# Attention ends one step sooner beside a pair, and the next pair's q, k, v are asked for in the step that it leaves

## Chip, cores and metric

The kernel runs on one core of one Trainium2 chip. The metric is the time of one execution on the device in microseconds (us), as the median of the runs of one kernel; lower is better.

## The reference, cut to what matters

```python
# 8 batches, 8 heads, 576 tokens, head width 64; chunks of 64 tokens
scores = scale * q_c @ k_c.T          # in each chunk of 64
attn = exp(scores - max); attn /= (sum + 1e-9)
out = attn @ v_c                       # heads joined: x is 4608 x 512
x = (x @ w_a * (x @ w_b)) @ w_out      # 512 -> 1536 -> 512
x = (x @ w1 * (x @ w2)) @ w3 @ w_out2  # 512 -> 1024 -> 1024 -> 512
```

All values are float32. w_a, w_b and the others come as 64-bit floats and are rewritten to float32 in the kernel.

## The kernel before, in words

The 4608 tokens are nine blocks of 512. Blocks 0 to 7 form four pairs (`sb` 0 to 3), block 8 is alone. Phase 0 is attention and the first gated product, phase 1 the second one. A product of float32 values is made of parts of fewer bits, three matmuls for one.

**Stages of phase 0.** Pair 0 goes through plain steps (`plain_step`): one step for each of the 12 slices of 128 hidden columns and each of the two blocks (T = 0 and 1), a pair of products `pa` and `pb` in each. A step with T = 0 also carries the second product (out of the hidden columns, into `acc`) of the slice before; the second products of the T = 1 block are left for a burst. Pairs 1 to 3 go through 12 Strassen steps each (`strassen_step`, `block_steps`): seven products of six matmuls for a slice of both blocks (P5, P1, P2, P6, P3, P7, P4 in this order), and 12 matmuls of the second product of the even block's slice before. The second product of the odd block follows in a burst (`burst`): 12 slices, called blocks of the burst in what follows, of four parts with three matmuls each, 144 matmuls in a row, and the four pending parts of the last step behind its first slice. In the burst the other engines also form the next pair's left factors (`strassen_pieces`).

**Attention.** A unit (`Unit`) is the attention of one block for two heads, eight units for a pair, four for block 8. Its pieces are load1 (q, k), load2 (v), turn (transposes of q and k), scores (32 small matmuls and the maximum), soft2, flip and flip2 (transposes), apply (32 small matmuls and the copies out). Units of pair 1 and before (`TurnedOnPE`) transpose through TensorE, the others on VectorE. `attention_pieces` writes the pieces of all units in one list with a cost for each, and a `Track` spreads the list over a number of points: at each `point()` it lets out pieces until their cost has reached the share of points passed. A Strassen step has 7 points, a burst gives one for each of its slices 4 to 11, a plain step 3 (T = 1) or 5 (T = 0). `finish()` lets out what is left. Attention beside pair 1 is that of pair 2, beside pair 2 that of pair 3, beside pair 3 that of block 8 (there with rewriting of weights, and without points in the burst).

**Loads.** q, k and v are not loaded where a unit asks for them: `ask` puts each small DMA on a list, and `tick(loads=n)` issues the next n of them on SP's queue: 3 ahead of each Strassen product, 1 ahead of each part of a second product (`Second.part`), 2 ahead of each plain product. `settle` issues at once whatever a unit needs by then: a turn calls it for its q and k, an apply for its v. SP also issues the weights (`load_part`, w, two steps ahead) and the second product's weights (`Outs.ahead`, wo, two slices ahead in a step, three in a burst, from four buffers), all in the order of the program. q, k and v have two buffers each, so the first two units of a pair can be loaded ahead (`attention_begins`) when the last two of the pair before have used theirs.

**The lines that matter.** `attention_begins` is called at line 1359, ahead of the burst; for pair 1 the first unit's 16 loads are then issued at once (line 1361). The spread is set in lines 1364 to 1372:

```python
n_pts = PTS * steps + steps - 4      # 7 * 12 + 8 points
at.append(Track(work, n_pts - 3))    # 89
```

In the plain phase the tail of the attention of pair 1 is spread over `4 * (len(order) - n) - 2` points from the first T = 1 step on, which is 82.

Of the kernel before, what the change touches and what calls it, by code (L numbers as in the profile page):

```python
# [78 lines left out]
def chunk_attention_two_gated_products(  # L79
# [66 lines left out]
    def settle(n):  # L146
        while asks["done"] < n and asks["left"]:
            nc.sync.dma_start(*asks["left"].popleft())  # L148
            asks["done"] += 1
# [89 lines left out]
    state = {"banks": ("rB", "rD")}  # L239
# [742 lines left out]
    def ready(ph, j, f, gplaces):  # L982
        return g_parts(gplaces[f // 4][:, f % 4], f"{ph}_{j}b{f}", nc.gpsimd)
# [44 lines left out]
    def attention_begins(units):  # L1028
        for u in units[:2]:
            u.load1()  # L1030
            u.load2()
# [61 lines left out]
    with tc.manual_schedule():  # L1093
# [54 lines left out]
        def unit_list(sb):  # L1148
            js = [LONE] if sb == NSB else [2 * sb, 2 * sb + 1]
            cls = TurnedOnPE if sb == 1 else Unit  # L1150
            return [cls(j, hp, T) for T, j in enumerate(js) for hp in range(NHP)]


        U = [First(T, hp, T) for T in range(2) for hp in range(NHP)]
        for i in range(3):
            pump.load(slot(6), nc.scalar)
# [45 lines left out]
        for n, (T, f) in enumerate(order):  # L1202
            if T == 0:
                conv = Track([conv_piece()] * (1 if f == 0 else 3), 5 if f + 1 < AHEAD else 8)
                if f + 1 == NF[0]:
                    conv = None
            if T == 1 and f == 0:
                late.finish()
                at = Track(both[cut:], 4 * (len(order) - n) - 2)

            def point(pe=True):
                if conv:
                    conv.point(pe)
                (at or late).point(pe)

            if n + 1 == len(order):
                state["ready"] = ready(0, 1, 0, plain[0])
            plain_step(0, 0, T, f, f"0_{T}_{f}", point, plain[0], sums[0], "AC")
            if conv and (T == 1 or f + 1 < AHEAD):
                conv.finish()  # L1220
                pump.flush()
# [17 lines left out]
        def block_steps(ph, sb, x, at):  # L1239

            single = sb == NSB
            j = LONE if single else 2 * sb
            nm = f"{ph}{sb}"
            new = ph == 0 and sb == 1
            whole_new = ph == 1 and sb == 0
            sums, gplaces = [], None if single else []
            n = NF[ph]
            su = first_sums
            last = single
            for f in range(n):  # L1250
                extra = None
                if new:
                    if f + 2 < n:
                        su[f + 2] = summed(ph, f + 2, f + 2)
                        su[f + 2].load()
                    extra = Track(su[f + 1].pieces() if f + 1 < n else [], 5)
                if whole_new:
                    if READY <= f + 2 < n:
                        su[f + 2] = Sums(ph, f + 2, dict(tag=f"Y{f % 2}"))
                        su[f + 2].load()  # L1260
                    if READY <= f + 1 < n:
                        extra = Track(su[f + 1].all_pieces(), 6)

                def freed(i):
                    if f + 2 < n:
                        if whole_new and f + 2 >= READY:
                            return
                        if not new or i in (0, 3):
                            load_part(ph, f + 2, i)
                    elif ph == 0 and sb + 1 == NSB:  # L1270
                        if i < 2:
                            load_plain(ph, f + 2 - n, i)
                    elif not last:
                        load_part(ph, f + 2 - n, i)

                def point(pe=True):
                    if extra:
                        extra.point()
                    for a in at:
                        a.point(pe)  # L1280

                if f + 1 == n and not single:
                    state["ready"] = ready(ph, j + 1, 0, gplaces)
                wo = state["outs"].next()
                strassen_step(ph, j, f, x, f"{nm}_{f}", point, gplaces, sums, wo, freed)
                if extra:
                    extra.finish()
            for a in at:
                a.finish()
            return j, gplaces  # L1290
# [44 lines left out]
        for ph, sb in [(0, sb) for sb in range(1, NSB + 1)] + [(1, sb) for sb in range(NSB + 1)]:  # L1335
            lone = ph == 0 and sb == NSB
            begins = ph == 1 and sb == 0
            if begins:
                state["outs"] = Outs(1, 2 * NSB + 1)
            state["outs"].ahead(2)  # L1340
            if lone:
                x, pieces = lone_pieces(x32, f"{ph}{sb}")
                pieces = pieces + o2_pieces()
                pump.cap = len(pump.jobs)
                slots["n"] = -1
                pieces += [(0.1, False, lambda: pump.load(slot("L")))] * 2
            elif not begins:
                x, pieces = strassen_pieces(x32, f"{ph}{sb}", sb == NSB)
            if ph == 0 and sb == 1:
                for f in range(2):  # L1350
                    first_sums[f] = summed(ph, f, f)
                    first_sums[f].load()
                for f, i in ((0, 0), (0, 3), (1, 0)):
                    load_part(ph, f, i)
                pieces = pieces + first_sums[0].pieces()
            steps, at, conv = NF[ph], [], []
            if ph == 0 and not lone:
                units = unit_list(sb + 1)
                attention_begins(units)
                if sb == 1:  # L1360
                    settle(units[0].qk_end)
                    load_part(ph, 1, 3)
                work = attention_pieces(units)
                n_pts = PTS * steps + steps - 4
                if sb == NSB - 1:
                    pump.cap += 3 * NF[1]
                    pump.load(slot(3))
                    pump.load(slot(3))
                    conv = later_conv(3 * NF[1], 3)
                    work = merged((0, 1, work), (0, 1, conv))  # L1370
                    n_pts = PTS * steps
                at.append(Track(work, n_pts - 3))
            if not begins:
                burst(ph, j + 1, places, pieces, [] if conv else at, state.pop("ready", None))
            if lone:
                got = []
                for n_ in range(4):
                    load_w3(n_)
                at.append(Track(between(got), 5 * steps - 15))
                xs = {}  # L1380

                def next_x():
                    diffs = deque()
                    for i in range(2):
                        t = pool.tile([P, 4, NT], F32, tag=f"G{i}", name=f"xd{i}")
                        diffs.extend(t[:, n_] for n_ in range(4))
                    xs["x"], xs["pieces"] = strassen_pieces(got, "10", diffs=diffs)

                early = [(0.1, False, lambda: (at[0].finish(), next_x()))]
                early += [(0.7, False, lambda n_=n_: xs["pieces"][n_][2]()) for n_ in range(18)]  # L1390
                late = Track(early, 11)
                class After:
                    n = 0

                    def point(self, pe=True):
                        self.n += 1
                        if self.n > 5 * steps - 15:
                            late.point(pe)

                    def finish(self):  # L1400
                        late.finish()

                at.append(After())
                lone_steps(ph, x, at)
                for p in xs["pieces"][18:]:
                    p[2]()
                x32, x = got, xs["x"]
                continue
            if ph == 1 and sb < NSB:
                got = []  # L1410
                js = [LONE] if sb == NSB - 1 else [2 * sb + 2, 2 * sb + 3]
                at.append(Track(x2_pieces(js, got), PTS * steps - 3))
            j, places = block_steps(ph, sb, x, at)
            if ph == 0:
                x32 = [u.x32 for u in units]
            elif sb < NSB:
                x32 = got
# [47 lines left out]
```

## Time and profile before

| | us |
|---|---|
| median of 3 runs | 1654.66 (1654.49 to 1661.31) |
| profiled execution, its own time | 1660.61 |
| its span, first to last instruction | 1658.8 |
| TensorE busy | 1568.2 |
| VectorE busy | 852.7 |
| plain steps, to about | 269 |
| burst, then pair 1 | 269 to 311, to 479 |
| burst, then pair 2 | 479 to 522, to 685 |
| burst, then pair 3 | 685 to 727, to 893 |
| burst, block 8, phase 1 | 893 to 932, to 1095, to 1659 |

Times in the profile are microseconds from the span's start. PE is TensorE, PEld its weight loads, DVE VectorE, ACT ScalarE, POOL GpSimd, SP the engine that issues most DMAs (SPq its queue of issues). L829 is the Strassen product, L858 the second product, L148 the issue of a q, k or v load, L701 of wo, L713 and L715 of w, L467 and L480 transposes through TensorE, L345 the scores, L396 the product with v. In brackets behind an instruction stands how long its engine was idle before it, and what ended that. The granted clock is a share of TensorE's full 2.4 GHz.

### The profile page before, as it was taken

How to read it: one execution, taken by the hardware profiler on the slowest of the kernel's cores; microseconds unless marked ns; L12 is line 12 of the kernel's file. 1: busy time of each engine (PE TensorE's matmuls, PEld its weight loads, DVE VectorE, ACT ScalarE, POOL GpSimd, SP SyncE). 2: the span in 40 equal slices, each digit the busy share in tenths (PEclk: the TensorE clock that was granted, in tenths of full speed). 3: DMA queues.
4: the chain of work that ended last, by engine and by line, in shares of the span. 5: the costliest groups of instructions: out<-in, count | busy, mean ns of one | idle time of the engine just before them, and what ended most of it. 6: DMA issues, size and time to landing. Idle time of an engine off the chain costs nothing.

```text
span 1658.8 us, 24429 instructions
## 1 busy us (share of the span) xinstructions
PE 1568.2 (95%) x8968; PEld 1256.4 (76%) x8968; DVE 852.7 (51%) x1384; ACT 551.8 (33%) x989; POOL 489.7 (30%) x502
## 2 busy tenths in 40 slices
PE   5789999899999999899999899999999999999998
PEld 4568777677776777677777677788878878878887
DVE  5657755777865455645676234544452352342331
ACT  5544444332242222332234222333332332331322
POOL 1213333222252111432224211223432331331432
PEclk8889999999999999999999999999999999999999
DMA  8768876878777777788986888886776676666684
GB/s 222 225 197 268 254 234 190 255 243 240 229 222 212 213 219 211 214 232 299 321 299 216 295 308 303 311 289 247 249 236 213 218 237 211 223 227 200 219 292 160
DMA packets 289975, 400.37 MB, mean 241 GB/s; under 512 B 175680, under 2 KB 196160, under 8 KB 289856
## 3 DMA queue, kind: packets, MB, share of 16 engines
q1 hardware_dynamic: 262688, 309.67, 61.3%
q0 software_dynamic: 23616, 81.80, 12.8%
q10 hardware_dynamic: 3552, 7.34, 1.2%
q8 instruction: 71, 1.16, 0.3%
q14 instruction: 48, 0.39, 0.1%
HBM read 312.74 MB, written 85.98 MB: 240 GB/s over the span
## 4 chain that ended last, share of the span: by engine, by line
PE 75%; DMA 7%; DVE 6%; issue 4%; ACT 3%; SPq 2%; POOL 2%; POOLq 0%; ACTq 0%; DVEq 0%
PE P L829 38%; PE acc L858 19%; PE pa L815 4%; PE pb L815 4%; PE wf L1082 3%; SPq L148 2%; PE pb0L L815 2%; PE pa0L L815 2%; DMA wo<-dwo 2%; PE x L396 1%; DMA cv_w<-in_moe_w_dram 1%; DVE xP L243 1%; DMA qk<-in_q_dram 1%; DMA cv_o<-in_moe_w_out_dram 1%; DVE c L917 1%
## 5 line engine op out<-in xcount | busy, mean ns | idle before, releaser
L829 PE MATMUL P<-xP,w 128*128 128x512 f32 (+1 forms) x3102 | 715.3, 383 | 19.9 <-DVE c L917 12.5
L829 PEld LDWEIGHTS P<-xP,w 128*128 128x128 f32 x3102 | 557.2, 188 | 147.2 <-DVE c L917 18.0
L917 DVE TENSOR_TENSOR c<-P,c 128x512 f32<-128x512 f32 (+1 forms) x228 | 150.5, 662 | 333.2 <-PE P L829 332.2
L914 ACT COPY c<-P 128x512 f32<-128x512 f32 (+1 forms) x228 | 128.6, 564 | 226.4 <-PE P L829 226.1
L945 POOL TENSOR_TENSOR G<-c,c 128x512 f32<-128x512 f32 x68 | 89.4, 1315 | 337.9 <-DVE c L917 337.8
L242 ACT CAST gh<-c 128x512 fp32r<-128x512 f32 x68 | 42.3, 622 | 329.7 <-DVE c L944 329.7
L243 POOL TENSOR_TENSOR gl<-c,gh 128x512 fp32r<-128x512 f32 x68 | 90.2, 1327 | 177.4 <-ACT gh L242 177.4
L858 PE MATMUL acc<-gh,wo 128*128 128x512 f32 x384 | 139.1, 400 | 0.0
L944 DVE TENSOR_TENSOR c<-P,c 128x512 f32<-128x512 f32 x68 | 47.0, 691 | 136.0 <-PE P L829 136.0
L858 PE MATMUL acc<-wo,gh 128*128 128x512 f32 x320 | 111.2, 391 | 0.5 <-ACT gh L242 0.5
L858 PEld LDWEIGHTS acc<-gh,wo 128*128 128x128 f32 x384 | 72.9, 190 | 16.6
L243 DVE TENSOR_TENSOR xP<-xP,xP 128x512 fp32r<-128x512 f32 (+1 forms) x56 | 64.2, 1187 | 25.3 <-ACT xP L242 25.2
L815 PE MATMUL pa<-xq,w 128*128 128x512 f32 x288 | 76.1, 416 | 0.0
L858 PE MATMUL acc<-gl,wo 128*128 128x512 f32 x192 | 75.6, 394 | 0.0
L157 POOL DMA_DIRECT2D dw<-w x58 | 32.5, 560 | 133.0 <-DVE w L243 79.2
L815 PE MATMUL pb<-xq,w 128*128 128x512 f32 x288 | 71.1, 396 | 0.0
L858 PEld LDWEIGHTS acc<-wo,gh 128*128 128x128 f32 x320 | 60.1, 188 | 13.9 <-ACT gh L242 1.0
L815 PEld LDWEIGHTS pa<-xq,w 128*128 128x128 f32 x288 | 57.1, 201 | 13.1
L867 ACT COPY ev<-acc 128x512 f32<-128x512 f32 x72 | 42.4, 589 | 71.8 <-PE acc L858 67.0
L858 PE MATMUL acc<-wo,gl 128*128 128x512 f32 x160 | 63.0, 394 | 0.8 <-POOL gl L243 0.8
L815 PEld LDWEIGHTS pb<-xq,w 128*128 128x128 f32 x288 | 53.0, 188 | 10.9
L1082 PE MATMUL wf<-wo,w3t 128*128 128x512 f32 x192 | 50.2, 421 | 4.8 <-DVE w3t L243 4.6
(154 smaller groups left out, 2327.2 us busy)
## 6 DMA issues: line engine op xcount, KB each, us to landing
w<-dw SPq DMA_DIRECT2D x213, 512.0 KB, 4.3
wo<-dwo SPq DMA_DIRECT2D x168, 512.0 KB, 4.5
dw<-w POOLq DMA_DIRECT2D x58, 512.0 KB, 4.8
w<-dw SPq DMA_DIRECT2D x87, 256.0 KB, 3.4
d<-cv POOLq DMA_DIRECT2D x40, 256.0 KB, 4.7
su<-d SPq DMA_DIRECT2D x20, 512.0 KB, 5.5
cv_o<-in_moe_w_out_dram SPq DMA_DIRECT2D x18, 512.0 KB, 5.8
x2d<-ev POOLq DMA_DIRECT2D x36, 256.0 KB, 4.8
```

The source lines that it names most:

```text
L148: nc.sync.dma_start(*asks["left"].popleft())
L242: nc.scalar.copy(dst_h, src)
L243: eng_l.tensor_tensor(dst_l, src, dst_h, op=ALU.subtract)
L815: nc.tensor.matmul(ps, w[m][:, kk // 2, wp, kk % 2], xq[kk // 2][:, kk % 2, xp], start=(n == 0), stop=(n == 3 * KM - 1),)
L829: nc.tensor.matmul(ps, w[:, wp, kt], x[:, kt, xp], start=(begins and n == 0), stop=(n == 5), skip_group_check=True,)
L858: nc.tensor.matmul(acc[m], a, b, start=(f == 0 and (wp, gp) == SEQ[0]), stop=(f == NF[ph] - 1 and (wp, gp) == SEQ[-1]),)
L867: nc.scalar.copy(t, acc[m])
L914: nc.scalar.copy(t, src)
L917: add = lambda o, a, b: nc.vector.tensor_tensor(o, a, b, op=ALU.add)
L944: nc.vector.tensor_tensor(g, last, c11, op=ALU.mult)
L945: nc.gpsimd.tensor_tensor(g_place(ph, nm.split("_")[0], f, gplaces), c22, c12, op=ALU.mult)
L1082: nc.tensor.matmul(ps, t[:, gp, jj], wo2[jj // 2][:, jj % 2, wp], start=(jj == 0 and (wp, gp) == SEQ[0]), stop=(jj == NF[1] - 1 and (wp, g ...
```

## The change

The first two units of the next pair are made, and their loads asked for, in a function of its own. It is called ahead of the last plain step and ahead of the last Strassen step of pairs 1 and 2, behind a `finish()` of the attention that runs there. The spread is shortened to fit: 78 points in the plain phase, 84 in pairs 1 and 2; pair 3 keeps its 81. The 16 loads that were issued at once ahead of the first burst no longer are.

```diff
+        def next_units(sb):
+            state["units"] = unit_list(sb)
+            attention_begins(state["units"])
...
-                at = Track(both[cut:], 4 * (len(order) - n) - 2)
+                at = Track(both[cut:], 4 * (len(order) - n) - 6)
...
             if n + 1 == len(order):
+                at.finish()
+                next_units(2)
                 state["ready"] = ready(0, 1, 0, plain[0])
...
+                if f + 1 == n and ph == 0 and sb + 1 < NSB:
+                    for a in at:
+                        a.finish()
+                    next_units(sb + 2)
                 if f + 1 == n and not single:
                     state["ready"] = ready(ph, j + 1, 0, gplaces)
...
             if ph == 0 and not lone:
-                units = unit_list(sb + 1)
-                attention_begins(units)
+                units = state.pop("units")
                 if sb == 1:
-                    settle(units[0].qk_end)
                     load_part(ph, 1, 3)
                 work = attention_pieces(units)
-                n_pts = PTS * steps + steps - 4
+                n_pts = PTS * (steps - 1) + steps - 4
...
-                at.append(Track(work, n_pts - 3))
+                at.append(Track(work, n_pts - 1 if sb + 1 < NSB else n_pts - 3))
```

## Rows read from the trace of the kernel before

**Rows 1.** The page, busy time by engine: us (share of the span) xinstructions.

```profile
PE 1568.2 (95%) x8968; PEld 1256.4 (76%) x8968; DVE 852.7 (51%) x1384; ACT 551.8 (33%) x989; POOL 489.7 (30%) x502
```

**Rows 2.** By stretch: length, busy PE, PEld, DVE, ACT, POOL, clock, DMA share, GB/s.

```profile
479.40:522.30 42.90, 39.18 (x191) 30.67 (x190) 32.27 (x38) 18.66 (x34) 21.90 (x18) 0.96 0.78 208
...
515.70:522.30 6.60, 4.63 (x14) 3.54 (x14) 2.36 (x5) 1.71 (x3) 1.11 (x2) 0.74 0.72 191
685.40:727.20 41.80, 37.28 (x160) 29.10 (x159) 26.63 (x27) 18.36 (x33) 21.96 (x18) 1.00 0.90 256
697.00:704.00 7.00, 3.52 (x16) 2.87 (x16) 7.00 (x9) 2.13 (x5) 3.04 (x2) 1.00 0.93 246
...
311.00:479.00 168.00, 161.45 (x1115) 125.96 (x1114) 115.09 (x215) 49.75 (x95) 45.29 (x49) 1.00 0.77 236
522.40:685.00 162.60, 159.80 (x1114) 126.06 (x1113) 79.75 (x152) 38.51 (x72) 32.18 (x26) 1.00 0.73 211
```

**Rows 3.** Timeline of TensorE, burst ahead of pair 2: start, length, instruction, [idle before].

```profile
494.09 0.47 PE L858 MATMUL acc<-gh_3b,wo 128*128 128x512 f32 x1 [0.51 <-DMA wo<-dwo]
...
512.87 0.47 PE L858 MATMUL acc<-gh_3b,wo 128*128 128x512 f32 x1 [0.27 <-DMA wo<-dwo]
...
517.84 0.60 PE L858 MATMUL acc<-gh_3b,wo 128*128 128x512 f32 x1 [1.96 <-DMA wo<-dwo]
```

**Rows 4.** Timeline of TensorE, burst ahead of pair 3.

```profile
700.57 0.47 PE L858 MATMUL acc<-gh_5b,wo 128*128 128x512 f32 x1 [3.48 <-DMA wo<-dwo]
```

**Rows 5.** Waits of TensorE in 311 to 479: us in total, times, longest.

```profile
PE P L829 <- DVE c L917: 3.7, 3, 1.8
PE x L396 <- DVE pT L384: 2.2, 3, 1.2
```

**Rows 6.** Waits of TensorE in 522.4 to 685.

```profile
PE P L829 <- DVE c L917: 2.5, 3, 1.1
```

**Rows 7.** Timeline of TensorE, end of the plain steps.

```profile
231.26 0.69 PE L396 MATMUL x<-pT,v 64*64 64x64 f32 x32 [1.00 <-ACT pT L483]
...
268.55 0.79 PE L396 MATMUL x<-pT,v 64*64 64x64 f32 x32 [0.73 <-ACT pT L483]
```

**Rows 8.** Timeline of SP's issues, burst ahead of pair 2.

```profile
478.98 0.32 SPq L715 DMA_DIRECT2D w<-dw  x1
479.67 0.32 SPq L701 DMA_DIRECT2D wo<-dwo  x1
480.04 4.82 SPq L148 DMA_DIRECT2D qk<-in_q_dram  x8
484.96 0.38 SPq L701 DMA_DIRECT2D wo<-dwo  x1
...
508.50 2.88 SPq L148 DMA_DIRECT2D qk<-in_k_dram  x6
...
513.48 0.54 SPq L701 DMA_DIRECT2D wo<-dwo  x1
```

**Rows 9.** Timeline of SP's issues, burst ahead of pair 3.

```profile
686.57 0.38 SPq L701 DMA_DIRECT2D wo<-dwo  x1
687.04 3.00 SPq L148 DMA_DIRECT2D qk<-in_q_dram  x4
690.08 4.57 SPq L148 DMA_DIRECT2D qk<-in_k_dram  x4
694.75 0.95 SPq L701 DMA_DIRECT2D wo<-dwo  x1
```

**Rows 10.** Instructions on the tile wo in 478 to 525, its loads.

```profile
DMA to landing us min/median/max: 3.6/4.7/6.2
```

**Rows 11.** Timeline of SP's issues, a step of pair 2 with 22 loads.

```profile
593.10 0.37 SPq L715 DMA_DIRECT2D w<-dw  x1
```

**Rows 12.** Timeline of TensorE, the same step.

```profile
586.45 1.66 PE L829 MATMUL P<-xP,w 128*128 128x512 f32 x6 [0.60 <-DVE c L917]
```

**Rows 13.** Timeline of SP's issues, plain steps.

```profile
227.84 2.80 SPq L148 DMA_DIRECT2D qk<-in_k_dram  x4
```

## The prediction

> **What bounds the kernel now.** I read the page first: TensorE is busy for 95% of the span [rows 1], so only its waits and its clock can be gained. Then I read the busy time by stretch, to find the stages next to the change, and in them TensorE's waits. Three stages matter. (a) The bursts, in which TensorE has only the second product of the odd block: 12 blocks of 12 matmuls, each block with its own weights wo. The burst ahead of pair 2 (479.4 to 522.3) and the one ahead of pair 3 (685.4 to 727.2) [rows 2] wait for wo: 0.51, 0.27 and 1.96 us in the one [rows 3], 3.48 us in the other [rows 4]. (b) The twelve-step stages of pairs 1 and 2, where TensorE waits for VectorE [rows 5, 6]. (c) The end of the plain steps, with a wait of 0.73 us ahead of the last attention product [rows 7].
>
> Why wo is late is read in SP's queue. SP issues everything in program order: wo, and among them the small loads of q, k, v, one at each accumulating part. In the burst at 479.4 the wo of block 2 is issued at 479.67, then eight q loads take 4.82 us, and block 3's wo goes out at 484.96; ahead of block 11's wo (513.48) stand eight more, six of them in 2.88 us [rows 8]. In the burst at 685.4 eight loads lie between 687.04 and 694.66, block 3's wo goes out only at 694.75, and that is the wait of 3.48 us [rows 4, 9]. A wo takes 3.6 to 6.2 us, in the median 4.7, from issue to landing [rows 10].
>
> **How late a wo may be.** Block 4 of the first burst would have started at 494.09 - 0.51 = 493.6; matmuls start every 0.22 us (16 in 3.52 us busy, [rows 2]), some 2.7 us for twelve, so block 3 was due at 490.9, 11.5 us after the stage's start, and block 2 one block sooner, 8.7. In the second burst block 3 was due at 697.1, 11.7 after the start, block 2 at 8.9 or a little less.
>
> **Part 1: what is moved.** Counted from the two load functions, a unit of a block that spans two batches (blocks 4 and 6) has 16 q and k loads and 10 of v, a unit of block 8 has 8 and 6. So 52 loads are asked for ahead of pair 2's and of pair 1's burst, 28 ahead of pair 3's. A Strassen step lets out 7 x 3 + 4 = 25 loads, a burst 52 (4 x 12, and 4 in the pending parts). Thus 25 of the 52 and 25 of the 28 go to the pair's last step; in the plain phase the last step has two products of 2 each, so 4. Nothing is removed: the same DMAs, bytes and SP time.
>
> What this costs in the last step: SP is free there now, its last weight load goes out at 478.98 as the step ends [rows 8]. A step with 22 loads ends otherwise: its last product begins at 586.45 and takes 1.66 us, and the weight load that this product frees is issued at 593.10, 5.0 us late [rows 11, 12]. 25 loads at 0.60 us (8 in 4.82) and five larger ones make 16.6 us against 12 us of matmuls (54 x 0.22): 4.6 late; at 0.48 us (6 in 2.88) 13.6, so 1.6 late [rows 8]. I take a lateness L of 4 us when the burst begins, between 1.6 and 5, nearer to the step that does what the new step will do. Those weights are needed only after the burst, so L matters to wo alone.
>
> **Burst ahead of pair 3.** Now 3 loads are left in it, not 28. Block 2's wo went out 1.2 us after the start [rows 9]; it goes out at L + 1.2 = 5.2 and lands at 9.9 to 11.0 (landing 4.7, or the 5.8 from 694.75 to 700.57). Due at 8.9 at the latest: a wait of 1.0 to 2.1, say 1.6. Block 3's follows at 5.2 + 0.4 + 3 x 0.6 = 7.4, lands at 12.1 to 13.2, due at 11.7 + 1.6: none. Before 3.48, after 1.6: **-1.9 us** (between -3.5 at L = 1.6, and -0.9 at L = 5).
>
> **Burst ahead of pair 2.** It has 27 of the 52 left, but from its sixth block the third unit's 16 q and k loads are asked for as now, so 43 of the 52 slots stay in use: the burst is hardly lighter until its last two blocks. Block 3's wo goes out at L + 0.4 + 4.8 = 9.2, lands at 13.9 to 15.0, due at 11.5: it waits about 3.0 us where it did not wait at all (the burst at 685.4 shows this case: issued 9.35 us after its start, 3.48 us of waiting). What goes: the waits 0.51 + 0.27 + 1.96 = 2.74 us, and the slow clock behind the last of them, where 14 matmuls took 4.63 us at a granted clock of 0.74 [rows 2], 1.55 us over 14 x 0.22. The eight loads ahead of block 11's wo become four, since the second unit's loads were all let out before its transposes force them. By block 3 alone the sum is 3.0 - 4.3 = -1.3. By SP's own pace it is less: from block 3's wo to block 11's SP took 28.5 us; with L = 4 in front and four loads (2.4 us) fewer, block 11's wo is 1.6 us later than before, which eats the 1.55 us of the clock. I take **-0.6 us**, from -4.0 (L = 1.6) to +1.8 (L = 5 and a slow clock again). The clock is no sure term: behind the longer wait of 3.48 us the stretch 697 to 704 kept 1.00 [rows 2].
>
> The Trainium skill, "DMA: Bandwidth & Descriptors", section "Issuing engines are not separate DMA queues", says that the time to initiate a DMA is usually small relative to the DMA itself. By that rule neither the old place nor the new one would cost anything. The trace disagrees: 9.35 us pass before one wo can be issued, against a median landing of 4.7 us. By the rule both burst terms would be nought.
>
> **Part 2: the earlier end of attention.** In the plain phase the spread falls from 82 points, of which only 81 exist, to 78. The tail behind the last product (a transpose through TensorE, a copy, 32 small matmuls with the 0.73 us wait [rows 7]) moves into the step before: -0.7. Against it, the last unit's turn comes one and a half steps sooner, to the end of the step that now ends with the attention product at 231.26 [rows 7]. That unit's k loads are issued until 227.84 + 2.80 = 230.6 [rows 13]; with a landing like wo's least, 3.6 us, they are there at 234.2, and TensorE, in order, would wait at about 232: 2.2 us; nothing if the counts let them go 2 loads earlier and the 1 us wait that is there now absorbs the rest. I take +1.3, together **+0.6 us** (-0.7 to +1.7).
>
> In pairs 1 and 2 the spread goes from 89 points to 84, 6% denser, and the last step has none. Scores, transposes, sums and products are the same number and keep their length. What can change is how often a piece stands in VectorE's queue ahead of an add that TensorE needs: the waits are 3.7 + 2.2 us in the one stage [rows 5] and 2.5 in the other [rows 6], 8.4 in all; 6% of them is 0.5. I take **+0.6 us**, between -2 and +3, since each wait is a coincidence of a piece and a product, and all of these shift.
>
> **Part 3: the forced issue.** Ahead of pair 1's burst 16 loads were forced out together; now 12 of them are spread in it. In the old place SP stood waiting for a weight buffer anyway, and that burst used all 52 slots before and uses 52 after. I put it at nothing; cover is the second unit's transposes, which now find their last load just issued instead of 12 loads ahead. Without cover VectorE waits one landing, up to 4.7 us, and TensorE only what is left of it at the next scores: 0 to 1 us.
>
> **Sum.** -1.9 - 0.6 + 0.6 + 0.6 = -1.3 us. It is made against the profiled execution, 1660.61 us with a span of 1658.8 (1.8 us around it); that one is 6.0 us above the median of the runs, 1654.66. I take the difference off the median: 1653.4 us.
>
> **The rivals.**
> A. Bursts clean (18%): L is near 1.6, because the last step has no attention and no loads waiting for buffers, which the 22-load step had. Then -3.5, -4.0 and the tail's -0.7: -8.2, so 1646.5 us. For it: VectorE and SP have nothing else in that step; against it: 25 x 0.60 us does not fit into 12 us.
> B. Slower (27%): SP's lateness is carried into the burst and grows. The place is the first blocks of both bursts, the price 1 us per us of L in each. It decides from L = 5.3 in the first burst (L - 1.0 against 4.3) and about 5.9 in the second; at L = 8 the two are +2.7 and +2.1, with the 1.2 of part 2 +6.0: 1660.7 us. For it: the step with only 22 loads already ends 5.0 us late; against it: that step began with loads waiting for buffers.
> C. Nothing moves (5%), as if issue time were free: both burst terms nought and part 2 nought, 1654.7 us. Against it stands the 3.48 us behind eight loads.
> The forecast, between -5 and +1.5, has 50%.
>
> **Range.** 1645 to 1661 us takes in A's and B's prices and all but about 2 in 10; the forecast's own range is 1649.5 to 1656. A measurement can tell some 0.5%, 8.3 us, from no change. Over 0.5% faster needs A and a gain in the pair stages too: 10%. Over 0.5% slower needs B at L = 8 and worse pair stages: 7%. Within: 83%.
>
> **What would show it.** Right: 25 q, k, v loads in the last step of pairs 1 and 2, the last weight load there some 4 us behind its product; no wait of about 3.5 us at block 3 of the burst ahead of pair 3, but one of 1 to 2 us at block 2; in the burst ahead of pair 2 a wait near block 3, none of 2 us at block 11; a wait for k at the last unit's turn near 232 us. Wrong: bursts without any wait for wo (A), bursts that are longer than 42.9 and 41.8 us (B), or stages of pairs 1 and 2 that differ by over 3 us from 168.0 and 162.6 [rows 2].

## The result, and the profile after

The changed kernel takes 1672.07 us in the median (1665.81 to 1673.06, 5 runs) against 1654.66 in the same job: a ratio of 1.0081, interval [1.0059, 1.0102], so 13.4 us slower (9.8 to 16.9, the ratio times 1654.66). Forecast were 1653.4 us and a range of 1645 to 1661; "slower by over 0.5%" had been given 7%. The profiled execution has a span of 1671.0 us, 12.2 more than before. TensorE is as busy as it was, so the time is waits and clock:

```profile
PE 1569.8 (94%) x8968; PEld 1258.9 (75%) x8968; DVE 850.4 (51%) x1384; ACT 551.6 (33%) x989; POOL 487.3 (29%) x502
```

Stage by stage, from the first matmul of a stage to the first of the next, in us (worked out from TensorE's timelines):

| stage | before | after | the kernel before once more (e8) |
|---|---|---|---|
| to the end of the plain steps | 269.3 | 273.4 | 267.6 |
| burst, pair 1 | 41.6, 168.6 | 41.6, 172.8 | 41.9, 168.6 |
| burst, pair 2 | 42.8, 163.4 | 45.6, 159.7 | 40.9, 163.5 |
| burst, pair 3 | 41.4, 166.9 | 45.7, 169.8 | 40.5, 165.6 |
| burst, block 8, phase 1 | 38.1, 162.9, 563.8 | 39.0, 159.4, 564.0 | 37.8, 163.0, 563.7 |

The plain steps, pairs 1 and 3 and two bursts lost 3 to 4 us each; pair 2 and the stage of block 8 won 3.7 and 3.5. (The 2.9 us in pair 3 are not explained; in the other traces here it takes 165.1 to 168.1.) The busy time by stretch answers [rows 2]; columns as there. In order: the burst ahead of pair 2 and the stretch behind its wait; the burst ahead of pair 3, its wait and the stretch behind it; pairs 1 and 2; a stretch in pair 1.

```profile
487.90:533.50 45.60, 39.05 (x189) 30.32 (x188) 30.76 (x38) 18.65 (x34) 19.93 (x18) 0.93 0.79 221
502.00:510.00 8.00, 7.48 (x25) 5.62 (x26) 5.03 (x8) 2.32 (x5) 1.30 (x1) 0.81 0.82 212
693.20:738.90 45.70, 37.12 (x157) 30.27 (x156) 26.55 (x27) 18.24 (x33) 19.79 (x18) 0.93 0.75 237
704.00:710.00 6.00, 0.00 (x0) 0.00 (x0) 6.00 (x8) 0.65 (x2) 1.80 (x2) 0.70 0.97 344
710.00:720.00 10.00, 9.87 (x37) 8.06 (x38) 4.13 (x4) 2.81 (x5) 2.75 (x2) 0.84 0.63 224
315.00:487.80 172.80, 163.48 (x1117) 127.98 (x1117) 116.76 (x215) 50.06 (x95) 45.41 (x49) 0.99 0.78 233
533.60:693.20 159.60, 159.28 (x1117) 126.56 (x1116) 81.24 (x153) 38.60 (x73) 32.43 (x27) 1.00 0.73 207
396.00:406.00 10.00, 6.71 (x24) 5.22 (x23) 7.62 (x13) 1.21 (x2) 2.64 (x2) 0.83 0.72 226
```

**The bursts.** TensorE's timeline in the two bursts answers [rows 3, 4]: one long wait for wo in each, at the burst's block 2 (the 0.52 and 0.25 us ahead of pair 2 are at its blocks 4 and 8).

```profile
501.97 0.77 PE L858 MATMUL acc<-gh_3b,wo 128*128 128x512 f32 x1 [5.76 <-DMA wo<-dwo]
509.76 0.47 PE L858 MATMUL acc<-gh_3b,wo 128*128 128x512 f32 x1 [0.52 <-DMA wo<-dwo]
522.03 0.47 PE L858 MATMUL acc<-gh_3b,wo 128*128 128x512 f32 x1 [0.25 <-DMA wo<-dwo]
...
710.13 0.77 PE L858 MATMUL acc<-gh_5b,wo 128*128 128x512 f32 x1 [8.58 <-DMA wo<-dwo]
```

The wait of 1.96 us at block 11 is gone, as forecast, and two longer ones came in front. Why is in SP's timeline, which answers [rows 8, 9]: the last step of pair 1, then that of pair 2.

```profile
476.05 5.40 SPq L148 DMA_DIRECT2D qk<-in_q_dram  x8
481.50 0.43 SPq L148 DMA_DIRECT2D qk<-in_k_dram  x1
482.03 0.41 SPq L713 DMA_DIRECT2D w<-dw  x1
...
493.68 0.53 SPq L715 DMA_DIRECT2D w<-dw  x1
494.25 0.47 SPq L148 DMA_DIRECT2D v<-in_v_dram  x1
494.82 0.64 SPq L701 DMA_DIRECT2D wo<-dwo  x1
...
683.45 4.15 SPq L148 DMA_DIRECT2D qk<-in_k_dram  x4
...
700.43 0.95 SPq L715 DMA_DIRECT2D w<-dw  x1
701.42 0.59 SPq L148 DMA_DIRECT2D v<-in_v_dram  x1
702.06 1.17 SPq L173 DMA_DIRECT2D cv_o<-in_moe_w_out_dram  x2
703.33 0.38 SPq L701 DMA_DIRECT2D wo<-dwo  x1
```

The last weight load (L715) can go out when the step's last product frees its buffer; that product ended at 487.35 and 692.68; it goes out at 493.68 and 700.43. SP is 6.3 and 7.8 us late, and block 2's wo goes out 6.9 and 10.1 us after the bursts' starts (487.9 and 693.2). Of the 25 loads 24 stand ahead of that weight load; in SP's rows they take 15.2 us in the one step and 16.4 in the other, 0.63 and 0.68 each. Most issues take 0.3 to 0.7 us. The rest is waits of SP for earlier loads to land, in the one step above all (1.4 us for a wo is the longest), and single long issues: of the four k loads in 4.15 us, one took 2.31. On the chain of waits (start, length, what) these two wo also take longer than the median of [rows 10]:

```profile
494.82 7.02 DMA wo<-dwo
...
703.33 6.67 DMA wo<-dwo
```

The second of them is no longer than before the change. Behind two rewriting loads (L173), block 2's wo ahead of pair 3 took 6.2 to 8.8 us to land in every trace here; in the kernel before, for the one issued at 686.57:

```profile
DMA to landing us min/median/max: 6.7/6.7/6.7
```

Block 2's wo ahead of pair 2 landed in 3.9 to 5.2 us in the other traces.

Behind both waits TensorE's clock is low: 37 matmuls took 9.87 us in 710 to 720 at a granted clock of 0.84, 25 took 7.48 us in 502 to 510 at 0.81. In TensorE's timeline the first seven behind each wait start some 0.43 us apart, the following ones 0.23: half the clock, 1.2 of 2.4 GHz, and 1.5 us lost in each burst.

**Pair 1.** VectorE's transpose of k waits for its load, the add behind it in VectorE's queue is late, a product waits, and the clock falls to 0.83 in 396 to 406 (1.4 us on 24 matmuls). In the trace before VectorE never waited for q or k there. The product with v also waits longer for VectorE's transposes (L396, released by L384): 4.5 us in the five traces with 84 points beside pair 1, e1's among them, against 2.2 in the nine others [rows 5]. That part is the spread alone.

```profile
397.59 0.71 DVE L334 STREAM_TRANSPOSE kT<-qk 128x512 f32<-128x512 f32 x1 [3.16 <-DMA qk<-in_k_dram]
```

```profile
399.53 2.93 PE L829 MATMUL P<-xP,w 128*128 128x512 f32 x6 [3.29 <-DVE c L917]
```

**Plain steps.** Transposes through TensorE now wait in two places, each at the turn of a unit; the 0.73 us at the tail [rows 7] is still there, one step earlier. TensorE's waits in 105 to 269 us (total, times, longest):

```profile
PE t L467 <- issue: 3.7, 2, 2.1
PE x L396 <- ACT pT L483: 1.1, 3, 0.7
```

The first wait is 1.69 us at 153.51, the second 2.06 us at 236.89, the last unit's turn. The profile names no releaser ("issue"), but the records do: TensorE's weight loads stand at a semaphore of VectorE's until 236.84, and VectorE's first instruction L356 ends at 236.79. That is the subtraction that reads the first bank of the scores last, and in the kernel the transposes fill the same bank. The unit's last k load had landed at 235.25, 0.4 us after TensorE became idle. At 153.5 it is the same (L356 ends at 153.41, k landed at 144.6), and so it is in e9.

```profile
236.38 0.74 DVE L356 TENSOR_TENSOR e<-s,mx 128x256 f32<-128x256 f32 x2
236.89 1.06 PE L467 MATMUL t<-ident,qk 128*128 128x128 f32 x8 [2.06 <-issue]
```

So the denser spread put a turn right behind another unit's scores; the loads were in time. What that costs repeats closely: from the 101st matmul of the products `pa` and `pb` (L815, at 105 to 111 us) to the burst, TensorE takes 159.6 to 159.7 us in all eight traces with the old spread, 162.4 to 162.5 in four of the six with the new one. In e3 and e4 it takes 164.6 and 164.9, with a wait of 0.40 and 0.73 us for k besides. The plain part thus costs 2.8 us; the rest of the 4.1 us between the two traces lies ahead of that point.

### The profile page after: what moved, and what is told of

It reads as the page before. It is cut to its first block, busy times and chain, and to the rows that moved or that the text cites. A ratio compares the mean times of both kernels' runs of the same rounds, so it can differ in the third digit from the quotient of the medians.

```text
span 1671.0 us, 24413 instructions
## 1 busy us (share of the span) xinstructions
PE 1569.8 (94%) x8968; PEld 1258.9 (75%) x8968; DVE 850.4 (51%) x1384; ACT 551.6 (33%) x989; POOL 487.3 (29%) x502
## 4 chain that ended last, share of the span: by engine, by line
PE 76%; DMA 7%; DVE 5%; issue 4%; SPq 3%; ACT 3%; POOL 2%; POOLq 0%; ACTq 0%; DVEq 0%
PE P L829 38%; PE acc L858 20%; PE pa L815 4%; PE pb L815 4%; PE wf L1082 3%; SPq L148 3%; DMA wo<-dwo 3%; PE pb0L L815 2%; PE pa0L L815 2%; PE x L396 1%; DMA qk<-in_k_dram 1%; PE s L345 1%; DMA cv_w<-in_moe_w_dram 1%; DVE xP L243 1%; DVE c L917 1%
## 5 line engine op out<-in xcount | busy, mean ns | idle before, releaser
L815 PE MATMUL pa<-xq,w 128*128 128x512 f32 x288 | 76.3, 416 | 0.0
L815 PE MATMUL pb<-xq,w 128*128 128x512 f32 x288 | 70.5, 393 | 0.0
L815 PEld LDWEIGHTS pa<-xq,w 128*128 128x128 f32 x288 | 56.3, 200 | 12.8
L815 PEld LDWEIGHTS pb<-xq,w 128*128 128x128 f32 x288 | 53.3, 188 | 11.2
L362 ACT ACTIVATE e<-e 128x512 f32<-128x512 f32 x36 | 22.8, 633 | 98.5 <-DVE e L356 98.5
```

Source lines behind the costliest of these rows:

```text
L815: nc.tensor.matmul(ps, w[m][:, kk // 2, wp, kk % 2], xq[kk // 2][:, kk % 2, xp], start=(n == 0), stop=(n == 3 * KM - 1),)
```

## The experiments

Two theories stood after this. **T**: two costs, SP's lateness into the two bursts (with the fall of the clock behind the waits) and a denser spread whose pieces reach loads that have not landed (for the plain steps the records above speak against the second). **Rivals**: one of the two alone; the DMA engines too full in the last step, whatever the order of issue; stage differences that are chance. Each kernel was timed in five rounds beside the kernel before, but for e8. Microseconds beside a ratio are the ratio's excess times 1654.6.

**e1_spread: the spread of the change, loads in the old place** (against the changed kernel)

```diff
-                next_units(2)            # ahead of the last plain step
-                    next_units(sb + 2)   # ahead of the last Strassen step
+                next_units(sb + 1)       # ahead of the burst
                 units = state.pop("units")
                 if sb == 1:
+                    settle(units[0].qk_end)
```

> The shorter spread (78, 84 and 84 points) as in the change, the next pair's loads asked for in the old place ahead of the burst. Theory T (two costs: SP ends the last step late and so the bursts' wo comes late; and the denser spread meets loads that have not landed): the bursts are back at some 42.8 and 41.4 us (45.6 and 45.7 with the change), the end of the plain steps and pair 1 stay some 2 and 4 us longer than before; the whole 7 us under the changed kernel, 1662 to 1666. Rival R1 (all of the loss is the denser spread): no less than the changed kernel, 1668 to 1672. Rival R2 (all of the loss is the moved loads): back at the kernel before, 1654 to 1657.

Median 1657.41 us, ratio 1.0015 [0.9995, 1.0035]: +2.5 us. So some 11 of the 13.4 us are the moved loads (10.9, and by the two intervals 6 to 16). R1 falls; R2 is closer to the measured time than T, which had left too much with the spread (1662 to 1666). The costs of the spread are in the trace all the same: the plain steps end at 270.2 and pair 1 takes 172.5 us, but pair 2 with 160.7 gives most of that back. The burst ahead of pair 3 takes 43.2, with a wait of 3.28 us, so it did not come back to 41.4.

**e2_thin: one load ahead of each product in the last step** (against the changed kernel)

```diff
-        tick(loads=3)
+        tick(loads=state.get("per", 3))
...
                     next_units(sb + 2)
+                    state["per"] = 1
                 ...
                 strassen_step(ph, j, f, x, ...)
+                state["per"] = 3
```

> As the change, but in the last Strassen step of pairs 1 and 2 one load goes out ahead of each product instead of three, so 11 instead of 25; the rest stays for the burst. Theory T: SP is no more than 2 us late at the end of that step, the waits for wo in the first blocks of the bursts go from 5.8 and 8.6 us to under 2.5, the whole 5 to 8 us under the changed kernel. If the waits came from the number of loads in the burst and not from SP's lateness at its start, the burst ahead of pair 3, which then has 17 loads instead of 3, would be longer and not shorter.

Median 1656.43, ratio 1.0015 [0.9998, 1.0032]: +2.5 us, so 11 us under the change. The waits for wo in the two bursts (total, times, longest), first the one ahead of pair 2:

```profile
PE acc L858 <- DMA wo<-dwo: 0.4, 2, 0.2
...
PE acc L858 <- DMA wo<-dwo: 4.4, 2, 2.7
```

The bursts take 38.4 and 40.8 us. The second has 17 loads in it instead of 3 and is 4.9 us shorter than in the change: it is the lateness at its start that counts, not the number in it. One of its two waits is 2.66 us, a little over the 2.5 forecast. What is left over the kernel before lies in the plain steps and in pair 1 (175.8 us).

**e3_act: the last step's loads on ScalarE's queue** (against the changed kernel)

```diff
-            nc.sync.dma_start(*asks["left"].popleft())
+            state.get("askq", nc.sync).dma_start(*asks["left"].popleft())
...
                     next_units(sb + 2)
+                    state["askq"] = nc.scalar   # nc.sync again behind the step
```

> As the change, but the 25 loads of the last Strassen step of pairs 1 and 2 are issued on ScalarE's queue, so that the weight loads and wo on SP are not behind them; the same DMAs at the same time. If SP's order makes wo late (T1): the last weight load of the step goes out within 1 us of its product, block 2's wo 0.3 to 1.2 us after the burst's start, waits for wo in the first three blocks under 1.5 us, the whole 5 to 10 us under the changed kernel, unless ScalarE's copies come late by its own issues of about 0.5 us each. If the DMA engines themselves are full (T2): wo is issued early but lands 8 us or more after its issue, and the waits of 5.8 and 8.6 us shrink by less than a half.

Median 1671.07, ratio 1.0107 [1.0085, 1.013], +17.7 us: no gain. But the wait is another one. SP's issues, then TensorE and ScalarE at the burst ahead of pair 3:

```profile
491.04 0.32 SPq L701 DMA_DIRECT2D wo<-dwo  x1
...
695.80 0.32 SPq L715 DMA_DIRECT2D w<-dw  x1
696.16 0.91 SPq L173 DMA_DIRECT2D cv_o<-in_moe_w_out_dram  x2
697.49 0.33 SPq L701 DMA_DIRECT2D wo<-dwo  x1
```

```profile
707.52 0.79 PE L858 MATMUL acc<-gh,wo 128*128 128x512 f32 x1 [8.34 <-ACT gh L242]
```

```profile
693.64 7.15 ACTq L148 DMA_DIRECT2D qk<-in_k_dram  x4
704.85 1.95 ACTq L148 DMA_DIRECT2D v<-in_v_dram  x3
706.85 0.62 ACT L242 CAST gh<-c 128x512 fp32r<-128x512 f32 x1 [16.27 <-DMA wo<-dwo]
```

Block 2's wo goes out 0.8 and 1.2 us after the bursts' starts (490.3 and 696.3) and lands 4.5 and 7.3 us later; TensorE waits 0.51 us for wo in the one burst and none in the other, where the copy holds it up first. T1 holds for SP: without the loads in front wo has landed 8.5 us after the start of the burst ahead of pair 3, though the DMA engines are as full (a share of 0.97 in 697.5 to 704.8) as in the change, where it took 16.8. So full DMA engines were not what held it. The loads then block ScalarE: its copy gh stands behind them for 16 us (the row names a wo load, but the last v load's issue ends at 706.81, and the copy starts at 706.85), and TensorE waits 8.34 us for that. The lateness follows the queue that holds the loads.

**e4_pair1: pair 1 and its burst's loads as before, the rest as in the change**

```diff
-                if f + 1 == n and ph == 0 and sb + 1 < NSB:
+                if f + 1 == n and ph == 0 and sb == 2:
...
+                if sb == 2:
+                    next_units(3)
                 units = state.pop("units")
-                n_pts = PTS * (steps - 1) + steps - 4
+                n_pts = PTS * (steps - (sb > 1)) + steps - 4
```

(and 89 points beside pair 1)

> As the change, but beside pair 1 the spread is the old one (89 points) and the loads for pair 3's first units are asked for in the old place. Theory T: pair 1 takes some 168.5 us (172.8 with the change), the burst ahead of pair 2 some 42.8 (45.6); the burst ahead of pair 3 stays at 45 or more; the whole about 7 us under the changed kernel. If pair 1's longer time in the changed kernel's trace is an accident of that execution, pair 1 does not differ and the gain is the burst's 3 us alone.

Median 1664.5, ratio 1.0049 [1.0023, 1.0075], +8.1 us: 5.3 under the change. Pair 1 takes 170.2, the burst behind it 40.3, the burst ahead of pair 3 44.8 us with one wait of 7.6. So pair 1 with its last step holds some 5 of the 13 us; by the two intervals that is not clear of nothing. That pair 1's longer time is no accident is shown by the traces together: it takes 172.5 to 178.9 us in the five with 84 points, 168.6 to 170.8 in the nine with 89.

**e5_pair2: of the change only pair 2's part, with the thin last step**

```diff
+                if f + 1 == n and ph == 0 and sb == 2:   # against the kernel before
+                    for a in at: a.finish()
+                    next_units(sb + 2); state["per"] = 1
...
+                if sb < 3: next_units(sb + 1)
+                units = state.pop("units")
-                n_pts = PTS * steps + steps - 4
+                n_pts = PTS * (steps - (sb > 1)) + steps - 4
```

> The plain steps and pair 1 as before the change (82 and 89 points, loads for pairs 2 and 3 ahead of their bursts); beside pair 2 the shorter spread and the moved loads, but one load ahead of each product in its last step, as in e2_thin. Theory T (the loss is SP's lateness in two bursts, with TensorE's clock falling behind the waits, and the denser spread in the plain steps and in pair 1, where the loads do not keep up): nothing of the loss is left, pair 2 is some 160 us (163.4 before), the burst ahead of pair 3 some 40.8 (41.4 before), the whole 2 to 6 us under the kernel before, 1649 to 1653. Rival (the shorter spread costs by itself, wherever it is): pair 2 no shorter than before and the whole at or over 1655.

Median 1654.0, ratio 0.9994 [0.9974, 1.0013]. The whole loss is gone, as T says; the gain that was hoped for is not told from nothing. Pair 2 takes 161.3 us, the burst ahead of pair 3 42.1, with a wait of 2.78 us for wo.

**e6_late: the kernel before, SP made late by 12 loads ahead of one burst**

```diff
+                if sb == 3:
+                    settle(asks["done"] + 12)
```

> The kernel before, but 12 of the 28 loads ahead of pair 3 are issued at once ahead of that burst's first wo, so that SP is late by a known amount and nothing else is changed. Theory T (SP's order alone makes the wait): block 2's wo goes out some 7 to 8.5 us after the start instead of 1.2, TensorE waits 4 to 6 us at block 2 instead of 3.48 at block 3, and if the clock falls behind a wait of that length, another 1.7 to 3.4 us go; the burst takes 43 to 46 us (41.4 before), the whole 2 to 5 us more than before. Rival (what costs is how full the DMA engines are in the last step, not SP's lateness): the burst stays within 1 us of 41.4.

Median 1658.34, ratio 1.0025 [1.0008, 1.0043], +4.1 us; the burst takes 47.1 us, more than forecast. SP's issue of block 2's wo, TensorE behind it, and the busy time by stretch (columns as [rows 2]):

```profile
692.28 0.40 SPq L701 DMA_DIRECT2D wo<-dwo  x1
```

```profile
701.27 0.77 PE L858 MATMUL acc<-gh_5b,wo 128*128 128x512 f32 x1 [8.91 <-DMA wo<-dwo]
```

```profile
701.20:708.00 6.80, 6.43 (x19) 4.96 (x20) 0.65 (x1) 1.66 (x3) 1.13 (x1) 0.71 0.87 218
```

Nothing but the order on SP differs here, and the changed kernel's wait appears, with its clock: nine matmuls start some 0.43 us apart, 1.9 us lost. wo went out 8.2 us after the start (684.1), as forecast, and landed 8.8 us later, which was not: with the 6.7 us that this wo took in the kernel before, the wait would have been 6.8. So the order makes most of it.

**e7_sparse: the kernel before, a load ahead of every second part only in the burst ahead of pair 3**

```diff
-            tick(loads=1)
+            state["odd"] = not state.get("odd")
+            tick(loads=0 if state.get("thin") and state["odd"] else 1)
```

> The kernel before, but in the burst ahead of pair 3 a load goes out ahead of every second part only. Theory T: the wait of 3.48 us at block 3 is gone or under 1 us, the burst takes some 38 us (41.4), the whole 2 to 4 us less than before; no load is needed before that burst ends. If the two weight rewriting loads ahead of the burst are what makes wo late there, the wait stays over 2 us.

Median 1653.6, ratio 0.9996 [0.998, 1.0013]: no difference. The burst takes 39.95 us with a wait of 2.41 us for wo. Here the expectation failed: with half the loads in front, block 3's wo was asked for 4.9 us after the start instead of 9.0, but landed 8.7 us after that, where it took 5.7 before. SP's issues:

```profile
684.14 3.43 SPq L148 DMA_DIRECT2D qk<-in_q_dram  x4
687.66 3.21 SPq L701 DMA_DIRECT2D wo<-dwo  x1
```

The issue itself took 3.21 us. What held it, the two rewriting loads ahead of the burst or the q loads, this run does not tell; the rival is nearer than T for the wait that the kernel before has.

**e8_before: the kernel before, unchanged, once more**

> The kernel before, unchanged, for a second profiled execution: how far the same stage differs between two executions. If the stage times of one trace can be compared to 1 us, plain steps, pair 1, pair 2 and the bursts repeat 269.3, 168.6, 163.4, 41.6, 42.8 and 41.4 us to within 1 us; where they do not, differences of that size are not told from one trace.

1654.82 us; its stages are in the table above. Pairs 1 and 2 repeat to 0.1 us, the plain steps and the two bursts are 1.7, 1.9 and 1.0 us shorter, and the wait of 3.48 us in the burst ahead of pair 3 is 2.08 here. So a single trace tells bursts to some 2 us at best: over all traces with the loads in the old place the burst ahead of pair 2 takes 38.4 to 42.8 us (before, e1, e4 to e10), the one ahead of pair 3 40.5 to 43.8 (before, e1, e8 to e10). The 45.6 and 45.7 of the change lie outside. Over all kernels here in which pair 1 kept its old spread (e4 to e9, e11, e12) it takes 168.6 to 170.8.

**e9_plain: the plain part alone** (`next_units(2)` and 78 points, the pairs as before)

```diff
-                at = Track(both[cut:], 4 * (len(order) - n) - 2)
+                at = Track(both[cut:], 4 * (len(order) - n) - 6)
...
             if n + 1 == len(order):
+                at.finish()
+                next_units(2)
```

> Only the plain part of the change: 78 points, the attention ended and pair 2's first loads asked for ahead of the last plain step, none issued at once; pairs 1 to 3 as before. Theory T: a wait of 2 to 4 us at the transposes of the last unit near 235 us takes more than the tail gives back, the plain steps end 1 to 2.5 us later, the whole 1 to 3 us over the kernel before. Rival (this part is harmless, all of it lies in the pairs): no wait at those transposes and no more than 0.5 us.

Median 1659.05, ratio 1.0032 [1.0015, 1.0049], +5.3 us (2.5 to 8.1). The waits at those transposes are there as in the change (TensorE's waits in 105 to 268 us):

```profile
PE t L467 <- issue: 3.8, 2, 2.1
```

The trace ends the plain steps at 268.8 us, against 266.0 to 269.3 in the kernels with the old plain part (before, e5 to e8, e10 to e12). So the waits of 3.8 us are shown, and counted from the 101st product on, 2.8 us (159.6 to 162.4); the rest of the 5.3 is not located. They are waits for VectorE, as in the change, so T has the place here and not the reason, loads that have not landed; the whole, 5.3 us, lies above its 1 to 3.

**e10_pair1: pair 1's spread alone**

```diff
-                n_pts = PTS * steps + steps - 4
+                n_pts = PTS * (steps - (sb == 1)) + steps - 4 + 2 * (sb == 1)
```

> Only pair 1's spread is shortened from 89 to 84 points; all loads in the old place. Theory T: VectorE's transposes reach k loads that have not landed, one to two waits of 2 to 3.3 us in VectorE and as much at TensorE's products, and its clock falls behind one of them; pair 1 takes 171.5 to 175 us (168.6 to 170.2 before), the whole 2 to 5 us more. Rival (pair 1's longer time came from SP's late start into it): VectorE does not wait for q or k in pair 1, pair 1 stays at 168.6 to 170.5.

Median 1656.2, ratio 1.001 [0.9993, 1.0026], +1.7 us, under the 2 to 5 forecast and not clear of nothing. In its trace, of an execution 4.7 us above the median, pair 1 takes 174.3 us, and the mechanism is the one of the change, VectorE first and TensorE behind it:

```profile
437.45 0.71 DVE L334 STREAM_TRANSPOSE kT<-qk 128x512 f32<-128x512 f32 x1 [3.42 <-DMA qk<-in_k_dram]
```

```profile
438.79 1.70 PE L829 MATMUL P<-xP,w 128*128 128x512 f32 x6 [3.21 <-DVE c L917]
```

**e11_wofirst: the kernel before, no loads in a burst until block 3's wo is asked for**

```diff
-            tick(loads=1)
+            tick(loads=0 if state.get("hold") else 1)   # set at the start of a burst,
...                                                      # cleared behind its first block
```

> The kernel before, but in the bursts ahead of pairs 2 and 3 no load goes out until block 3's wo has been asked for. Theory T (order on SP makes wo late): the waits for wo of 2 to 3.5 us in the burst ahead of pair 3 fall under 1 us, the burst takes 37 to 39 us (40.5 to 41.4), the burst ahead of pair 2 keeps or loses 1 us; the whole 2 to 5 us under the kernel before. Rival (wo is late because of what else is on the DMA engines at that time): waits for wo stay over 2 us at a later block.

Median 1656.66, ratio 1.0014 [1.0002, 1.0026], +2.3 us (0.3 to 4.3): no faster, if anything a little slower. The long wait at block 3 is gone, and later ones take its place: in the burst ahead of pair 3 four waits for wo of 1.2 us and less (2.8 in all) and two for ScalarE (1.5); in the burst ahead of pair 2 one of 2.78 us at its end and 1.74 for the transposes. The bursts take 42.9 and 41.6 us. A burst must pass all its loads somewhere; holding them back gained nothing here.

**e12_best: e11 with pair 2's spread at 84 points**

```diff
-                n_pts = PTS * steps + steps - 4      # against e11_wofirst
+                n_pts = PTS * (steps - (sb == 2)) + steps - 4 + 2 * (sb == 2)
```

> As e11_wofirst, and pair 2's spread at 84 points, with the loads in the old place. Pair 2 took 159.6 to 161.3 us in all kernels with that spread against 162.5 to 164.7 with the old one. Theory T: pair 2 at some 160.5, the whole 4 to 8 us under the kernel before, 1646 to 1650. If pair 2's shorter time is only taken from the stage ahead of it or given back in the burst behind it, no more than e11_wofirst brings.

Median 1653.62, ratio 0.999 [0.9972, 1.0009]: not told from the kernel before. Pair 2 takes 159.8 us, with waits of 0.2 us for VectorE's add against 2.5 [rows 6]. The expectation was careless in one point: the 162.5 us it gives to the old spread are e4's, which has the new one, and e3 with 164.1 has it too; the old one took 163.4 to 164.7. The shorter spread suits pair 2 by 2 to 4 us where nothing else disturbs the stage. No kernel here beats the kernel before clearly.

## Why the prediction was wrong

**The counts were right, the lateness was not.** 25 loads in the last step, the first blocks of the bursts as the place, block 11's wait gone: all as written. The step that failed first is "I take a lateness L of 4 us when the burst begins, between 1.6 and 5". L is 6.3 and 7.8. The working had 16.6 us of SP's time against 12 us of matmuls. From the first load to the last weight load SP took 17.6 and 19.0 us, and it had 11.3 us, since the first load goes out 0.6 us into the step and the last product ends 0.5 us ahead of the burst. So the 0.60 us a load was near (0.63 and 0.68); the 4 us was taken below the working's own 4.6, and the bound of 5 came from a step with 22 loads, and was taken as an end where it was a middle.

**The price was the second step.** Ahead of pair 2 the sum had 3.0 us for block 3 ("block 3's wo goes out at L + 0.4 + 4.8") and no term for block 2, whose wo now stood behind the loads as well. TensorE waited 5.76 us at block 2, and 0.52 + 0.25 later. Ahead of pair 3 the sum had 1.6 us; measured are 8.58. With the measured L its formula, L - 2.4, gives 5.4 us. Of the other 3.2, about 1.4 are the landing of 6.67 us where 4.7 to 5.8 were taken from other wo, 1.1 that wo went out 10.1 us after the start instead of L + 1.2, and 0.6 that block 2 was due at 8.3. The trace of the kernel before already had 6.7 us for that very wo. So rival B, "the price 1 us per us of L in each", had the mechanism and the sign, and was too cheap.

**The clock was left out of it.** "The clock is no sure term" was argued from one wait of 3.48 us that kept 1.00. Behind the waits of 5.76, 8.58 and, in e6, 8.91 us the stretches have 0.81, 0.84 and 0.71, and cost 1.5, 1.5 and 1.9 us. The 1.55 us taken off for block 11 came back elsewhere. The page "TensorE: Matmul & The Clock Gate" of the Trainium skill, section 'Part 1: The HAM clock gate (the "warmup" mystery)', has the throttled state as the default that activity releases; what followed these three waits agrees.

**Part 2 had the place and not the size.** The plain part was put at +0.6 (-0.7 to +1.7): it measured 2.8 us in the traces, and e9 has +5.3 us (2.5 to 8.1). The forecast wait of 2.2 us for k at the last unit's turn is there with 2.06 us, but that is luck: k had landed 1.6 us before the wait ended, and what ended it was VectorE. A second wait of the same kind, 1.69 us at another turn, was not foreseen. For pairs 1 and 2 "+0.6" was worked out as 6% of waits of 8.4 us. That was the wrong kind of sum: pair 1 got a new wait, VectorE on a k load (3.16 us), and 2.3 us more ahead of the products with v, and e10 has +1.7 us (-1.2 to 4.3) for it, 174.3 us in its trace; pair 2 won 2 to 4 us in five of the seven traces with that spread (not in e3 and e4). Part 3, the forced issue, held as far as the traces tell: the burst ahead of pair 1 takes 41.6 us before and after.

**Issue time counts.** The prediction set the trace against the page "DMA: Bandwidth & Descriptors" of the Trainium skill, section "Issuing engines are not separate DMA queues", by which the time to initiate DMAs is usually small. For a single DMA the traces agree: 0.63 and 0.68 us a load in SP's rows of the two last steps, against a median landing of 4.7 for a wo [rows 10]. Of a row of them ahead of one load that is waited for, that sentence says nothing, so it was no forecast of a free issue. The row of issues does count: in e6 only the order on SP was changed, by 12 issues, and it cost 4.1 us (1.3 to 7.1).

**The account.** Of 13.4 us some 11 are the 25 loads in two last steps (the change against e1, and again against e2); the spread as a whole is +2.5 (-0.8 to +5.8), in which pair 2's gain stands against pair 1 and the plain steps (2.8). By places, pair 1 with its last step holds 5.3 (the change against e4), an interval that reaches to nothing. Open stay what makes single issues on SP take 1.3 to 3.2 us, why block 2's wo ahead of pair 2 landed in 7.0 us instead of 3.9 to 5.2, pair 3's 2.9 us in the changed trace, and the part of e9's 5.3 us beyond 2.8.

## What to carry to other kernels

A queue that issues in program order is a resource with a length: before small DMAs are moved into a step, set their measured issue times, at the slow end, against the time from the first of them to the step's end, and ask which late consumer stands behind them, and how long its own load takes to land in that place. Where a wait falls where it was forecast, look at who ended it before the forecast is called right. Price a new wait on TensorE with the slow stretch behind it, not by its length alone. Moving work to an emptier place gained nothing here where the same queue serves both places; letting out 11 loads there instead of 25 took the loss away.

## What was not expected of the hardware

An issue on ScalarE's queue holds its arithmetic: with 25 loads on it a copy was idle for 16.27 us (e3). The granted clock is not told by the length of the wait alone: 1.96 us was followed by 0.74, 3.48 us by 1.00 [rows 2 to 4]. A single wo took 3.21 us to issue behind four loads (e7), where others take 0.32. And the stage of block 8, which no kernel here touched, took 159.1 to 161.0 us in some traces and 162.6 to 163.0 in the others, so that a difference of 3 us in one stage of one trace can be nothing.
